# Small adds and the first batch's routing on GpSimd, four low parts of run 0's weight chunks on VectorE, in a fused attention, expert and feed-forward kernel

## The chip, the core and the metric

One core of one Trainium2 chip. The metric is the device time of one execution in microseconds (us); the time of a kernel is the median of its runs. TensorE (PE) does the matrix products and transposes, VectorE (DVE) and ScalarE (ACT) the elementwise work, GpSimd (POOL) elementwise work out of SBUF and the indirect DMAs, SyncE (SP) issues the other DMAs. Each engine takes its instructions in program order and waits on semaphores for the others.

## What is computed

Three layers behind each other. Attention: 2 batches of 8 heads, 576 positions, head size 64, with rotary embedding of q and k. Then a mixture of 8 experts over the 1152 tokens of 512 values, of which each token takes two. Then a feed-forward layer with softplus. The routing of the experts, on which this change bears, is

```
logits = x @ w_gate
noise_scale = np.log1p(np.exp(x @ w_noise))
noisy_logits = logits + noise_scale * noise
top2 = np.argpartition(-noisy_logits, 2, axis=1)[:, :2]
...
h = np.maximum(x[mask] @ w1[e], 0.0)
out[mask] += top2_w[mask, k, None] * (h @ w2[e])
```

## The kernel before, in words

**The attention stage** takes 16 heads g (8 per batch, batch 0 first) in 8 pairs p. A head has five row blocks, so there are 80 blocks n. For each, PE makes the scores S (L462), DVE the row maximum M (L475), ACT the exponential E with the row sums (L483). PE transposes the result (T, L496 to L508), ACT writes the high part of the transpose (L518) and DVE the rest as low part (L448). PE multiplies by the values (A, L532), ACT copies that out (L540 to L543), and PE forms X (L554): the head's output rows and its share of the 16 logits of every token. DVE scales X by the reciprocal row sum into `lgt` (L564) and `xs` (L573); the reciprocal comes from `row_sum` (L559, L560), two DVE instructions on 128x5 values for each head. Before a pair can start, its q and k are rotated on POOL (`rope_op`, ten instructions, L366 to L395) and transposed on PE (prep, L422 to L433), and its values are split on POOL (L402, L403).

**The routing** of batch 0 runs inside the attention of batch 1, as steps of the generator `route(0)` between two yields each, nearly all on DVE: sums over the heads (`presum`, L586, L587), softplus (L683 to L687), the two largest of 8 logits (L692 to L697), `Mt` and `Ms0`, which mark and count the chosen experts (L699, L702), counts over tokens on PE (RP, L706), positions (L718 to L732), `choose` for the expert of run 0 (L603 to L608), keys, indicator tiles `ohA` (L748) and `ohB` (L751, L753), a second product on PE (RP2, L758) and the index lists (L762, L763). `choose_rest` on POOL (L612 to L619) ends with `ordA`, the number of the expert of run 0, which SP must read before it can load that expert's weights. With `idxA` POOL gathers the rows of run 0 (`gather_A`, L919); PE transposes them (XT, L938).

**Weights.** `load_chunk` (L152) brings a chunk of 512 KB into one of four `wraw` buffers. `split_hi` (L170, ACT) writes its high part; the second half, queued in `lo_q`, subtracts it for the low part (L174) and then issues the next load into a free buffer. Run 0 needs eight chunks; the first six are split inside the attention stage, their low parts on POOL. Chunks 4 and 5 can be loaded only when the buffers of chunks 0 and 1 are free, that is when their low parts are done.

**After attention**, PE does run 0: `gemm1` (L250 to L252), between its halves the counts of the other batches' routing (`route(1)`, on DVE from L672), then `gemm2`, then a branch on `mxi` (L1284), and runs 1 to 8 and the feed-forward layer follow.

**The order of the attention stage** is made when the kernel is built. Each step is an `op` with a key, an engine, an assumed cost in ns, a place, and the steps it comes after; the table `AHEAD` shifts the place of each kind. `schedule` takes steps one by one, always the one that can start soonest by the assumed costs, lower place first, and writes out their instructions in that order. Two rows that matter later:

```
op(("rs", g), "DVE", 300, n - 3, [("E", 5 * g + 4)], row_sum, g)
op(("sl", i), "POOL", 2300, 100, [("sp", i)], lambda: lo_q.pop(0)())
```

Of the kernel before, what the change touches and what calls it, by code (L numbers as in the profile page):

```python
# [103 lines left out]
def fused_kernel(ctx: ExitStack, tc: tile.TileContext, q, k, v, w_gate, w_noise, noise, w1, w2,  # L104
# [55 lines left out]
    def split_hi():  # L160
# [8 lines left out]
        lo_eng = nc.gpsimd if s < NWA else nc.vector  # L169
# [413 lines left out]
    def presum(b):  # L583
        V = nc.vector
        if b == 0:
            V.tensor_reduce(out=Lx, in_=lgt[:, 4].rearrange("p h o -> p o h"), axis=AX.X, op=OP.add)  # L586
            V.tensor_reduce(out=L0, in_=lgt[:, 0:4].rearrange("p t h o -> p t o h"), axis=AX.X, op=OP.add)  # L587
        else:
            V.tensor_reduce(out=L1, in_=lgt[:, 5:10, 0:H - 2].rearrange("p t h o -> p t o h"), axis=AX.X, op=OP.add)
            V.tensor_tensor(out=L1[:, 0], in0=L1[:, 0], in1=Lx, op=OP.add)  # L590
            V.tensor_tensor(out=L1, in0=L1, in1=lgt[:, 5:10, H - 2], op=OP.add)

# [7 lines left out]
    def choose():  # L600

        V = nc.vector
# [55 lines left out]
    def route(b, pool):  # L658
        t0, t1 = (0, 4) if b == 0 else (4, NT)
# [4 lines left out]
        def tmp(name, shape, dt=F32):  # L664
            return pool.tile([128] + shape, dt, name=f"{name}{b}")

        if b == 0:
            presum(b)
            L = L0
        else:  # L670
            L = L1
            V.tensor_tensor(out=L, in0=L, in1=lgt[:, 5:10, H - 1], op=OP.add)  # L672
# [40 lines left out]
        if b == 0:  # L713
            nc.tensor.matmul(ps[:, NT, :], ones, Ms0, start=True, stop=True)
# [12 lines left out]
        if b:  # L727
            V.scalar_tensor_tensor(out=kc, in0=ps[:, NT, :], scalar=8.0, in1=kb2, op0=OP.mult, op1=OP.add)
            rank_steps = ranks(pool)
            next(rank_steps)  # L730
        else:
            V.scalar_tensor_tensor(out=kA, in0=ps[:, NT, :], scalar=8.0, in1=kb, op0=OP.mult, op1=OP.add)  # L732
            yield
            choose()
            yield
        V.tensor_tensor(out=pr, in0=oh[:, ts], in1=(tbB if b else tbA)[:, None, None, :].to_broadcast([128, T, 2, E]),
                        op=OP.mult)
# [811 lines left out]
```

## Time and profile before

| what | value |
|---|---|
| median of 3 runs | 676.83 us (675.26 to 677.0) |
| the profiled execution's own time | 676.09 us |
| its span, first to last instruction | 674.3 us |
| busy share of the span: PE, DVE, ACT, POOL | 94%, 76%, 64%, 34% |
| TensorE's granted clock, mean | 0.994 |

The profile is one execution. Its times count from the span's start. The attention stage lies from 0 to about 198 us. PE's busy time takes in the tails of its matmuls, so short waits of PE are hidden in it.

### The profile page before, as it was taken

How to read it: one execution, taken by the hardware profiler on the slowest of the kernel's cores; microseconds unless marked ns; L12 is line 12 of the kernel's file. 1: busy time of each engine (PE TensorE's matmuls, PEld its weight loads, DVE VectorE, ACT ScalarE, POOL GpSimd, SP SyncE). 2: the span in 40 equal slices, each digit the busy share in tenths (PEclk: the TensorE clock that was granted, in tenths of full speed). 3: DMA queues.
4: the chain of work that ended last, by engine and by line, in shares of the span. 5: the costliest groups of instructions: out<-in, count | busy, mean ns of one | idle time of the engine just before them, and what ended most of it. 6: DMA issues, size and time to landing. Idle time of an engine off the chain costs nothing.

```text
span 674.3 us, 11714 instructions
## 1 busy us (share of the span) xinstructions
PE 636.9 (94%) x4066; PEld 569.7 (84%) x4066; DVE 509.9 (76%) x1063; ACT 432.8 (64%) x912; POOL 228.4 (34%) x241
## 2 busy tenths in 40 slices
PE   3999999889998999999999999988999999999997
PEld 2798989878987888979888898977789999889996
DVE  7889899999986558768677768655997655676665
ACT  2887888678873547747575765645876544565553
POOL 6968966772365301432313241322120100000000
PEclk9999999999999999999999999998999999999999
DMA  6318421001441868998999899884520100100000
GB/s 157 92 44 308 137 56 55 1 19 55 144 130 55 289 216 261 322 345 282 354 303 315 290 315 318 279 311 126 157 60 35 33 17 0 48 2 1 32 1 31
DMA packets 67901, 101.08 MB, mean 150 GB/s; under 512 B 11232, under 2 KB 38624, under 8 KB 67840
## 3 DMA queue, kind: packets, MB, share of 16 engines
q1 hardware_dynamic: 61552, 84.59, 38.5%
q0 software_dynamic: 3136, 10.10, 4.6%
q10 hardware_dynamic: 3152, 5.62, 2.2%
q8 instruction: 33, 0.54, 0.3%
q14 instruction: 28, 0.23, 0.1%
HBM read 76.70 MB, written 23.59 MB: 149 GB/s over the span
## 4 chain that ended last, share of the span: by engine, by line
PE 62%; issue 2%; DMA 2%; DVE 1%; ACT 0%; POOL 0%; POOLq 0%; DVEq 0%
PE p L250 10%; PE p L251 10%; PE p L252 10%; PE ph L250 5%; PE po L252 5%; PE ph L251 5%; PE ph L252 5%; PE po L251 5%; PE po L250 5%; PE p L1117 2%; PE p L1119 2%; PE pa L1073 1%; DMA yg<-ytab,yrow 1%; DMA ytab<-y 1%; PE px L1366 0%
## 5 line engine op out<-in xcount | busy, mean ns | idle before, releaser
L174 DVE TENSOR_TENSOR w<-wraw,w 128x1024 fp32r<-128x1024 f32 x69 | 93.8, 1370 | 1.2 <-ACT w L170 1.2
L219 POOL TENSOR_TENSOR dm<-dm,da 128x512 int32<-128x512 int32 x32 | 42.0, 1314 | 134.0 <-DVE da L216 57.0
L170 ACT ACTIVATE w<-wraw 128x1024 fp32r<-128x1024 f32 x75 | 78.7, 1055 | 7.9 <-DMA wraw<-in_moe_w_dram 7.2
L251 PE MATMUL p<-xl,w 128*128 128x320 f32 (+3 forms) x256 | 77.5, 303 | 0.3 <-DVE xl L1076 0.3
L250 PE MATMUL p<-xh,w 128*128 128x320 f32 (+3 forms) x256 | 77.4, 302 | 0.0
L252 PE MATMUL p<-xh,w 128*128 128x320 f32 (+3 forms) x256 | 77.3, 302 | 0.0
L1427 ACT ACTIVATE fa<-ph 128x256 f32<-128x256 f32 (+1 forms) x64 | 26.0, 407 | 69.6 <-PE ph L252 69.5
L483 ACT ACTIVATE P<-ps,nmx 128x576 f32<-128x576 f32 (+1 forms) x80 | 59.2, 740 | 13.0 <-DVE nmx L475 11.9
L475 DVE TENSOR_REDUCE nmx<-ps 128x1 f32<-128x576 f32 (+1 forms) x80 | 60.0, 751 | 7.3 <-PE ps L462 5.8
L250 PE MATMUL ph<-xh,w 128*128 128x256 f32 (+1 forms) x192 | 58.4, 304 | 1.7 <-DVE xl L1372 1.4
L518 ACT ACTIVATE pth<-pt 128x512 fp32r<-128x512 f32 (+2 forms) x96 | 53.5, 569 | 9.3 <-PE pt L496 5.1
L250 PE MATMUL p<-w,hb 128*128 128x512 f32 x144 | 58.7, 408 | 0.0
L252 PE MATMUL ph<-xh,w 128*128 128x256 f32 (+1 forms) x192 | 57.4, 299 | 0.0
L251 PE MATMUL ph<-xl,w 128*128 128x256 f32 (+1 forms) x192 | 57.3, 299 | 0.0
L1093 DVE SCALAR_TENSOR_TENSOR hb<-p,hb 128x256 fp32r<-128x256 f32 (+1 forms) x104 | 31.7, 345 | 32.9 <-ACT hb L1089 32.8
L252 PE MATMUL p<-w,hb 128*128 128x512 f32 x144 | 56.6, 393 | 0.0
L251 PE MATMUL p<-w,hb 128*128 128x512 f32 x144 | 56.5, 393 | 0.0
L1434 DVE TENSOR_SCALAR fu<-fa 128x256 f32<-128x256 f32 (+1 forms) x64 | 19.8, 309 | 47.2 <-ACT fa L1428 46.9
L448 DVE TENSOR_TENSOR ptl<-pt,pth 128x512 fp32r<-128x512 f32 (+1 forms) x80 | 49.5, 628 | 2.0 <-ACT pth L518 1.5
L1347 POOL DMA_INDIRECT yg<-ytab,yrow x18 | 18.9, 1048 | 92.5 <-PE px L1366 71.6
L251 PEld LDWEIGHTS p<-xl,w 128*128 128x128 f32 x256 | 48.2, 188 | 0.8 <-DVE xl L1076 0.5
L250 PEld LDWEIGHTS p<-xh,w 128*128 128x128 f32 x256 | 48.2, 188 | 0.6 <-ACT xh L1075 0.2
(291 smaller groups left out, 1899.3 us busy)
## 6 DMA issues: line engine op xcount, KB each, us to landing
wraw<-in_moe_w_dram SPq DMA_DIRECT2D x64, 512.0 KB
x<-in_moe_w_in_dram SPq DMA_DIRECT2D x16, 512.0 KB
x<-in_moe_w_out_dram SPq DMA_DIRECT2D x16, 512.0 KB
wtab<-dm SPq DMA_DIRECT2D x32, 256.0 KB
wraw<-wtab SPq DMA_DIRECT2D x16, 512.0 KB
ytab<-y ACTq DMA_DIRECT2D x18, 256.0 KB
ytab<-zrow SPq DMA_DIRECT2D x1, 4096.0 KB
w<-in_v_dram SPq DMA_DIRECT2D x8, 256.0 KB
```

The source lines that it names most:

```text
L170: nc.scalar.activation(hi, r, AF.Copy)
L174: lo_eng.tensor_tensor(out=lo, in0=r, in1=hi.bitcast(F32), op=OP.subtract)
L219: nc.gpsimd.tensor_tensor(out=m, in0=m, in1=ai, op=OP.add)
L250: nc.tensor.matmul(ps, ah, bh, start=first and i == 0, stop=False)
L251: nc.tensor.matmul(ps, ah, bl, start=False, stop=False)
L252: nc.tensor.matmul(ps, al, bh, start=False, stop=last and i == n - 1)
L448: nc.vector.tensor_tensor(out=dl, in0=x, in1=dh.bitcast(F32), op=OP.subtract)
L475: nc.vector.tensor_reduce(out=nmx[p0:p1], in_=stS[n][p0:p1, :, :HN], axis=AX.XY, op=OP.max, negate=True)
L483: nc.scalar.activation(Pt[p0:p1, 0:S].rearrange("p (a c) -> p a c", a=2), ps[p0:p1, :, :HN], AF.Exp, bias=nmx[p0:p1], scale=1.0, accum_out ...
L518: nc.scalar.activation(*evac.pop(("T", g, u)), AF.Copy)
L1093: nc.vector.scalar_tensor_tensor(out=o, in0=ps[:, c], scalar=0.0, in1=hh[:, c].bitcast(F32), op0=OP.max, op1=OP.subtract)
L1427: nc.scalar.activation(a, ps, AF.Abs)
```

## The change

GpSimd now does the add of `row_sum` (the reciprocal stays on VectorE as `row_inv`), both `presum` functions (as trees of adds in place in `lgt`), and of the routing of batch 0 the softplus arithmetic, `Mt` and `Ms0`, `choose` after the maximum, the keys and both indicator tiles, of which it writes 8 and 8 rows with one instruction each. VectorE keeps the largest-two search and what reads PSUM. `route` now serves the other batches alone and is as before. Of run 0's first six low parts GpSimd keeps two and VectorE takes four. The chunk loads come after `choose_rest` instead of after the last routing step, and the first two high parts no longer wait for the last rotation. The rotation is given to the scheduler in nine pieces instead of one. `AHEAD` is unchanged.

```diff
-        lo_eng = nc.gpsimd if s < NWA else nc.vector
+        lo_eng = nc.gpsimd if s < 2 else nc.vector
...
     def row_sum(g):
         b, h = divmod(g, H)
-        nc.vector.tensor_scalar(rinv[:, b, :, h], sums[:, b, :, h], 1e-9, None, op0=OP.add)
+        nc.gpsimd.tensor_scalar(rinv[:, b, :, h], sums[:, b, :, h], 1e-9, None, op0=OP.add)
+
+    def row_inv(g):
+        b, h = divmod(g, H)
         nc.vector.reciprocal(rinv[:, b, :, h], rinv[:, b, :, h])
...
+        g = nc.gpsimd
+        t = lgt[:, 5 * b:5 * b + 5]
         if b == 0:
-            V.tensor_reduce(out=Lx, in_=lgt[:, 4].rearrange("p h o -> p o h"), axis=AX.X, op=OP.add)
-            V.tensor_reduce(out=L0, in_=lgt[:, 0:4].rearrange("p t h o -> p t o h"), axis=AX.X, op=OP.add)
+            g.tensor_tensor(out=t[:, :, 0:4], in0=t[:, :, 0:4], in1=t[:, :, 4:8], op=OP.add)
+            g.tensor_tensor(out=t[:, :, 0:2], in0=t[:, :, 0:2], in1=t[:, :, 2:4], op=OP.add)
+            g.tensor_tensor(out=L0, in0=t[:, 0:4, 0], in1=t[:, 0:4, 1], op=OP.add)
+            g.tensor_tensor(out=Lx, in0=t[:, 4, 0], in1=t[:, 4, 1], op=OP.add)
...
-        V = nc.vector
-        V.scalar_tensor_tensor(out=kA, in0=kA, scalar=8.0 * CAPS[0] + 8.0, in1=kA, op0=OP.is_lt, op1=OP.mult)
-        V.tensor_reduce(out=topA, in_=kA, axis=AX.X, op=OP.max)
-        V.tensor_scalar(isA, kA, topA[:, 0:1], None, op0=OP.is_equal)
...
+        g = nc.gpsimd
+        g.tensor_scalar(isA, kA, topA[:, 0:1], None, op0=OP.is_equal)
...
+    def route_first(pool):
...
+        g.tensor_scalar(c_, e_, 1.0, 1.0, op0=OP.add, op1=OP.subtract)
+        g.tensor_tensor(out=c_, in0=e_, in1=c_, op=OP.subtract)
+        g.tensor_tensor(out=l_, in0=l_, in1=c_, op=OP.add)
+        g.tensor_tensor(out=l_, in0=l_, in1=nz[:, ts], op=OP.mult)
+        g.tensor_tensor(out=nl, in0=l_, in1=L0[:, :, 0:8], op=OP.add)
...
+        g.tensor_tensor(out=Mt[:, ts], in0=oh[:, ts, 0], in1=oh[:, ts, 1], op=OP.add)
...
+                g.tensor_scalar(ohA[:, i, kk, :], iotaA, pmf[:, i, kk:kk + 1], None, op0=OP.is_equal)
...
+                g.tensor_scalar(ohB[:, i, kk, :], iotaB, key[:, i, kk:kk + 1], tval[:, i:i + 1], op0=OP.is_equal,
+                                op1=OP.mult)
...
-        op(("rs", g), "DVE", 300, n - 3, [("E", 5 * g + 4)], row_sum, g)
+        op(("rs", g), "POOL", 260, n - 8000, [("E", 5 * g + 4)], row_sum, g)
+        op(("ri", g), "DVE", 190, n - 60, [("rs", g)], row_inv, g)
...
-    op(("cr", 0), "POOL", 2300, 100, [("R", 7)], choose_rest)
+    op(("cr", 0), "POOL", 2300, 100, [("R", 8)], choose_rest)
...
-        op(("ld", i), "SP", 1500, 70 + i, [("Xd", 9), last[0]], load_chunk)
+        op(("ld", i), "SP", 1500, 70 + i, [("Xd", 9), ("cr", 0)], load_chunk)
...
-        op(("sl", i), "POOL", 2300, 100, [("sp", i)], lambda: lo_q.pop(0)())
-    op(("L", 0), "DVE", 1060, 80, [("Xd", 14)], presum, 1)
+        op(("sl", i), *(("POOL", 2400) if i < 2 else ("DVE", 1250)), 100, [("sp", i)], lambda: lo_q.pop(0)())
+    op(("L", 0), "POOL", 1700, 80, [("Xl", 14), ("R", 0)], presum, 1)
```

How the change moves instructions shows best at three places. The first is POOL's queue from the end of `choose_rest` on, as it was before (`wraw` is a loaded chunk, `w0` to `w5` the split chunks, `w5` also the gathered rows):

```order
L617 CAST ordA_90<-rank1_113 128x1
L618 TENSOR_SCALAR kb2_110<-isA_106 128x8
L619 TENSOR_TENSOR kb2_110<-kb2_110,kb_99 128x8
L919 DMA w5_2410<-xtab_60,idxA_87 128x512
L919 DMA w5_2410<-xtab_60,idxA_87 64x512
L174 TENSOR_TENSOR w0_2477<-wraw_2413,w0_2477 128x1024
L174 TENSOR_TENSOR w1_2565<-wraw_2443,w1_2565 128x1024
L174 TENSOR_TENSOR w2_2624<-wraw_2475,w2_2624 128x1024
```

and as it is with the change:

```order
L625 CAST ordA_90<-rank1_113 128x1
L626 TENSOR_SCALAR kb2_110<-isA_106 128x8
L627 TENSOR_TENSOR kb2_110<-kb2_110,kb_99 128x8
L559 TENSOR_SCALAR rinv_151<-sums_150 128x5
L736 TENSOR_SCALAR ohA0_2348<-iotaA_118,pmf0_2318 128x128 x8
L740 TENSOR_SCALAR ohB0_2349<-iotaB_119,key_84,tval_120 128x30 x8
L742 TENSOR_TENSOR dl8_80<-m80_2000 128x4
L559 TENSOR_SCALAR rinv_151<-sums_150 128x5
L990 DMA w5_2546<-xtab_60,idxA_87 128x512
L990 DMA w5_2546<-xtab_60,idxA_87 64x512
L174 TENSOR_TENSOR w0_2542<-wraw_2416,w0_2542 128x1024
L174 TENSOR_TENSOR w1_2588<-wraw_2453,w1_2588 128x1024
```

Sixteen indicator rows now stand between `ordA` and the gather, and two low parts instead of six behind it. On PE, RP comes after the scores of block 68 where it came after those of block 55, and RP2 after block 75 where it came after block 70.

The second place is ACT at the end of the attention stage, before (`P1` is the exponential of the last block, `pth` the high parts of transposes, `o0` and `o1` the outputs of the last two heads):

```order
L483 ACTIVATE P1_153,sums_150<-ps_2633,nmx_2647 64x576
L542 ACTIVATE o0_147<-pa_2649 128x224
L543 ACTIVATE o0_147<-pa_2649 128x64
L518 ACTIVATE pth_2593<-pt_2665 64x512
L518 ACTIVATE pth_2593<-pt_2670 128x4x128
L170 ACTIVATE w3_2688<-wraw_2499 128x1024
L518 ACTIVATE pth_2593<-pt_2691 128x5x64
L170 ACTIVATE w4_2714<-wraw_2512 128x1024
L540 ACTIVATE o1_148<-pa_2697 128x288
L170 ACTIVATE w5_2732<-wraw_2583 128x1024
L542 ACTIVATE o1_148<-pa_2721 128x224
L543 ACTIVATE o1_148<-pa_2721 128x64
```

and with the change:

```order
L483 ACTIVATE P1_153,sums_150<-ps_2631,nmx_2642 64x576
L170 ACTIVATE w2_2661<-wraw_2486 128x1024
L542 ACTIVATE o0_147<-pa_2650 128x224
L543 ACTIVATE o0_147<-pa_2650 128x64
L518 ACTIVATE pth_2624<-pt_2665 128x5x64
L518 ACTIVATE pth_2624<-pt_2672 128x4x128
L170 ACTIVATE w3_2694<-wraw_2508 128x1024
L540 ACTIVATE o0_147<-pa_2682 128x288
L170 ACTIVATE w4_2700<-wraw_2579 128x1024
L170 ACTIVATE w5_2711<-wraw_2608 128x1024
L518 ACTIVATE pth_2624<-pt_2713 128x4x128
L518 ACTIVATE pth_2624<-pt_2719 128x4x128
```

Four high parts of chunks instead of three now follow the last exponential, and all four stand ahead of the last two transposes' high parts.

The third place is DVE at the same point with the change (`pth` and `ptl` with a `pt` are the low parts of transposes):

```order
L174 TENSOR_TENSOR w2_2661<-wraw_2486,w2_2661 128x1024
L448 TENSOR_TENSOR ptl_2625<-pt_2672,pth_2624 128x4x128
L448 TENSOR_TENSOR ptl_2625<-pt_2665,pth_2624 128x4x64
L448 TENSOR_TENSOR pth_2624<-pt_2665,pth_2624 64x64
L174 TENSOR_TENSOR w3_2694<-wraw_2508,w3_2694 128x1024
L174 TENSOR_TENSOR w4_2700<-wraw_2579,w4_2700 128x1024
L567 TENSOR_TENSOR lgt_143<-pa_2705,rinv_151 128x5x16
L448 TENSOR_TENSOR ptl_2625<-pt_2713,pth_2624 128x4x128
L448 TENSOR_TENSOR ptl_2625<-pt_2719,pth_2624 128x4x128
L576 TENSOR_TENSOR xs_2744<-pa_2705,rinv_151 128x5x64
L174 TENSOR_TENSOR w5_2711<-wraw_2608,w5_2711 128x1024
```

None of the L174 rows stood on DVE in this stage before; three of the four are ahead of the last transposes' low parts.

## Rows read from the trace of the kernel before

**Rows 1.** Stretches, start:end, length; busy us and instructions of PE, PEld, DVE, ACT, POOL

```profile
34.00:51.00 17.00, 17.00 (x141) 16.45 (x140) 14.92 (x31) 14.12 (x37) 11.63 (x17) 1.00 0.18 51
...
54.30:114.07 59.77, 57.06 (x463) 54.42 (x462) 54.72 (x103) 49.44 (x125) 44.15 (x35) 1.00 0.42 138
114.07:171.34 57.27, 50.19 (x397) 45.48 (x395) 55.76 (x129) 42.31 (x104) 32.48 (x34) 1.00 0.16 49
```

**Rows 2.** Timeline of DVE, start and duration: one add of the routing

```profile
123.02 1.29 DVE L685 TENSOR_TENSOR l<-l,c 128x32 f32<-128x32 f32 x1
```

**Rows 3.** DVE in the eleven stretches that hold only moved instructions; last their sum

```profile
115.87:117.09 1.22, 1.22 (x3) 1.00 0.60 169
...
169.75:170.62 0.87, 0.81 (x3) 1.00 0.87 254
sum 11.88, DVE 11.43; mean DVE 1.04
```

**Rows 4.** Groups of DVE from 114.07 to 171.34 us: busy us, mean ns

```profile
L559 DVE TENSOR_SCALAR rinv<-sums 128x5 f32<-128x5 f32 x4 | 2.7, 663 | 0.0
...
L607 DVE TENSOR_TENSOR tbA<-isA,dA 128x8 f32<-128x8 f32 x1 | 1.4, 1383 | 0.0
...
L560 DVE RECIPROCAL rinv<-rinv 128x5 f32<-128x5 f32 x4 | 0.8, 191 | 0.1
...
L608 DVE TENSOR_TENSOR tbA<-tbA,base 128x8 f32<-128x8 f32 x1 | 0.2, 167 | 0.0
```

**Rows 5.** Groups from 0 to 270 us, all engines: busy us, mean ns, idle before

```profile
L518 ACT ACTIVATE pth<-pt 128x512 fp32r<-128x512 f32 (+2 forms) x96 | 53.5, 569 | 9.3 <-PE pt L496 5.1 <-PE pt L508 2.6 <-PE pt L500 1.1
...
L170 ACT ACTIVATE w<-wraw 128x1024 fp32r<-128x1024 f32 x23 | 24.3, 1056 | 2.9 <-DMA wraw<-in_moe_w_dram 2.8
L174 DVE TENSOR_TENSOR w<-wraw,w 128x1024 fp32r<-128x1024 f32 x17 | 21.9, 1300 | 0.0
...
L559 DVE TENSOR_SCALAR rinv<-sums 128x5 f32<-128x5 f32 x16 | 7.4, 460 | 1.4 <-ACT P L483 1.3
```

**Rows 6.** Groups of POOL over the whole span, shapes apart

```profile
L174 POOL TENSOR_TENSOR w<-wraw,w 128x1024 fp32r<-128x1024 f32 x6 | 14.2, 2389 | 11.2 <-ACT w L170 11.2
...
L1099 POOL TENSOR_TENSOR hb<-h,hb 128x128 fp32r<-128x128 f32 x6 | 2.8, 474 | 1.9 <-ACT h L1097 1.9
...
L619 POOL TENSOR_TENSOR kb<-kb,kb 128x8 f32<-128x8 f32 x1 | 0.2, 202 | 0.1
```

**Rows 7.** Timeline of POOL, start, duration, idle before with its releaser

```profile
122.80 1.47 POOL L384 TENSOR_TENSOR w<-w,w 128x576 f32<-128x576 f32 x1
...
125.56 1.46 POOL L395 TENSOR_TENSOR yg<-w,yg 128x576 fp32r<-128x576 f32 x1
...
172.56 1.24 POOL L919 DMA_INDIRECT w<-xtab,idxA  x1 [8.65 <-DVE dl L766]
174.09 0.91 POOL L919 DMA_INDIRECT w<-xtab,idxA  x1 [0.30 <-issue]
177.37 2.38 POOL L174 TENSOR_TENSOR w<-wraw,w 128x1024 fp32r<-128x1024 f32 x1 [2.37 <-ACT w L170]
```

**Rows 8.** Timeline of PE, start, duration, idle before with its releaser

```profile
136.13 0.63 PE L422 MATMUL pa<-ident,w 128*128 128x128 f32 x4
...
196.64 1.13 PE L554 MATMUL pa<-Wx,o 128*128 128x96 f32 x8 [0.90 <-ACT o L543]
...
204.21 0.20 PE L706 MATMUL pa<-Mt,tri 128*128 128x48 bf16 x1 [0.85 <-DVE Mt L699]
...
218.21 0.52 PE L1073 MATMUL pa<-ident,xg 128*128 128x128 f32 x3 [2.23 <-PEq L1284]
```

**Rows 9.** Timeline of ACT: the last exponential

```profile
189.97 0.74 ACT L483 ACTIVATE P<-ps,nmx 64x576 f32<-64x576 f32 x1
```

**Rows 10.** Stretches behind the first low part of a chunk, columns as in rows 1

```profile
181.20:183.20 2.00, 1.71 (x14) 1.47 (x14) 1.94 (x4) 1.98 (x7) 0.00 (x0) 1.00 0.67 250
183.20:187.00 3.80, 3.80 (x32) 3.57 (x31) 3.76 (x10) 3.62 (x9) 2.38 (x1) 1.00 0.00 0
```

More of the change, by code (lines that the diff above doesn't have):

```diff
@@ L660, in route @@
+    def route(pool):
+        t0, t1 = 4, NT
         T = t1 - t0
@@ L664, in tmp @@
         def tmp(name, shape, dt=F32):
[L665 to L672, printed above, removed]
+            return pool.tile([128] + shape, dt, name=f"{name}1")
+        L = L1
+        V.tensor_tensor(out=L, in0=L, in1=lgt[:, 5:10, H - 1], op=OP.add)
         e_ = tmp("e_", [T, E])
@@ L699, in route @@
         V.tensor_tensor(out=Mt[:, ts], in0=oh[:, ts, 0], in1=oh[:, ts, 1], op=OP.add)
-        if b == 0:
-            with nc.allow_low_precision("small integers, exact in bfloat16"):
-                V.tensor_reduce(out=Ms0, in_=Mt[:, 0:4].rearrange("p t e -> p e t"), axis=AX.X, op=OP.add)
         yield
         ps = psA.tile([128, NT + 1, E], F32, name="pa")
-        tn = t1 if b == 0 else NT + 1
+        tn = NT + 1
         nc.tensor.matmul(ps[:, t0:tn, :], tri, Mt[:, t0:tn, :], start=True, stop=False)
-        if b:
-            nc.tensor.matmul(ps[:, t0:tn, :], ones, Ms0[:, None, :].to_broadcast([128, tn - t0, E]), start=False,
-                             stop=False)
+        nc.tensor.matmul(ps[:, t0:tn, :], ones, Ms0[:, None, :].to_broadcast([128, tn - t0, E]), start=False,
+                         stop=False)
         for i in range(t0, tn - 1):
@@ L726, in route @@
         V.tensor_copy(out=pmf, in_=posm[:, ts])
[L727 to L737, printed above, removed]
+        V.scalar_tensor_tensor(out=kc, in0=ps[:, NT, :], scalar=8.0, in1=kb2, op0=OP.mult, op1=OP.add)
+        rank_steps = ranks(pool)
+        next(rank_steps)
+        V.tensor_tensor(out=pr, in0=oh[:, ts], in1=tbB[:, None, None, :].to_broadcast([128, T, 2, E]), op=OP.mult)
         ov = tmp("ov", [T, 2])
@@ L760, in route @@
         yield
-        if b == 0:
-            V.tensor_copy(out=idx0, in_=ps2)
-            V.tensor_copy(out=idxA, in_=ps2[:, E * CB:E * CB + RTILES[0]])
-        else:
-            V.tensor_tensor(out=idx, in0=ps2, in1=idx0, op=OP.add)
-        V.tensor_tensor(out=dl8[:, ts], in0=m8[:, :, 1], in1=m8[:, :, 0], op=OP.subtract)
-        if b:
-            yield
-            next(rank_steps)
-            yield
-            next(rank_steps)
+        V.tensor_tensor(out=idx, in0=ps2, in1=idx0, op=OP.add)
+        V.tensor_tensor(out=dl8[:, ts], in0=m8[:, :, 1], in1=m8[:, :, 0], op=OP.subtract)
+        yield
+        next(rank_steps)
+        yield
+        next(rank_steps)
     def later(pool):
@@ L985, in fused_kernel @@
         if p:
-            op(("rope", p), "POOL", 12800, n - 8, [("prep", p - 1, u) for u in range(5)] +
-               [("lp", p)] * (p > 2) if p > 1 else [("in", 0)], rope_op,
-               p)
+            after = [("prep", p - 1, u) for u in range(5)] + [("lp", p)] * (p > 2) if p > 1 else [("in", 0)]
+            pieces = list(rope_pieces(p))
+            for j, (cost, fn) in enumerate(pieces):
+                name = ("rope", p) if j + 1 == len(pieces) else ("ro", p, j)
+                op(name, "POOL", cost, n - 8 + (AHEAD["rope1" if p == 1 else "rope"] if j + 1 < len(pieces) else 0),
+                   after, fn)
+                after = [name]
         op(("vs", p), "POOL", 2850, n - 8, [("A", 2 * p - 3, 1), ("lv", p)] if p > 1 else [("in", 1)], vs_op, p)
```

130 lines of the change are left out of this document (98 added, 32 removed).

## The prediction

> **What bounds the kernel now.** The profile's page puts the end of the kernel on PE, so a gain has to come from PE waiting less. I looked at the busy time by stretches for the place where PE is less busy than elsewhere. In the attention stage between 54.30 and 114.07 us PE is busy 57.06 of 59.77 us and DVE 54.72; between 114.07 and 171.34 us, where the routing of batch 0 runs, PE falls to 50.19 of 57.27 us while DVE is busy 55.76 [rows 1]. The reader is to see that DVE has no time left there (97%) and that ACT, with 42.31, and POOL, with 32.48, have plenty. So DVE sets the pace of that stretch.
>
> Next I looked at what DVE does there. The group view shows small adds of very different price: 167 ns for one on 128x8, 1383 ns for its neighbour on the same shape [rows 4]. The timelines of DVE and POOL side by side say why: the add that starts at 123.02 us lasts 1.29 us, to 124.31, and a POOL instruction that was already running ends at 122.80 + 1.47 = 124.27 [rows 2, 7]. A small DVE instruction that reads and writes SBUF alone waits there for POOL's current one. The reciprocal, 191 ns on average, does not [rows 4].
>
> **What leaves DVE.** The sums over the heads, the softplus arithmetic, the marks, the choice, the keys and the indicator tiles fill eleven stretches of DVE's timeline with 11.88 us together [rows 3]. The four adds of `row_sum` in this stage add 2.7 us [rows 4]. That is 14.6 us of 57.27. What stays on DVE for the routing (the search for the largest two, the instructions that read PSUM) is moved later in the order and costs the same.
>
> What it is worth is set by the next engine. PE runs 397 instructions in the stretch. In the stretch before it ran 463 in 59.77 us, 0.129 us each [rows 1]; at that rate 397 take 51.2 us. Sixteen of them are the small products RP and RP2; without any charge for them it is 49.2. So the stretch would shrink by 6.0 to 8.1 us; **I take 7.2**. DVE alone would allow more: 55.76 - 14.6 = 41.2 us of work at the 92% of the stretch before is 45 us. The upper end is the densest stretch of the stage, 141 instructions in 17 us [rows 1], 0.121 each: 381 of them take 46 us, a gain of 11.3. The lower end is that ACT's and DVE's waits for each other keep half of it, 3.6.
>
> The other twelve adds of `row_sum` cost 7.4 - 2.7 = 4.7 us [rows 4, 5], spread over stretches where PE is 95% busy. **I take 1.0**, between 0 and 4.7, nearer the low end because little of PE's time is free there.
>
> **What POOL takes on.** Some 45 small instructions in the stretch, with no row of their own; the nearest are 202 ns for 128x8 and 474 ns for 128x128 [rows 6], so 9 to 21 us; most are of the small kind, and I take 13. With 32.48 us of its own POOL then holds 46 of about 50 us at most. That is covered as long as the rotation stays early: before, the rotation of pair 6 ended at 125.56 + 1.46 = 127.0 us and PE first used it at 136.13, 9 us later [rows 7, 8]. The two adds of `row_sum` per pair wait on POOL for an exponential, and the rotation is queued behind them; they and the sums over the heads take some 2 to 4 us of those 9. Cost nothing; if the cover went, each us would be a us of PE.
>
> An instruction of 128x1024 takes 2389 ns on POOL and 1300 on DVE [rows 5, 6], a factor of 1.8; for 128x8 it is 202 ns on POOL against 167 to 1383 on DVE [rows 4, 6]. The Trainium skill, page "GPSIMD Engine Reference", section "4.1 Engine selection", puts elementwise work on VectorE because GpSimd is about twice as slow with two inputs; by it this change would be wrong for the adds and right for the low parts, and the rows bear it out for the large shape only.
>
> **The end of the stage.** The first transposed rows of run 0 and the first low parts keep their kind and come later in the order. Four low parts go to DVE at 1.30 us [rows 5], 5.2 us, and lie in DVE's gaps while ACT works; the last sums over the heads, which DVE did there, go to POOL. The path is ACT's. Before, from the last exponential at 189.97 us to the last head's X at 196.64 passed 6.7 us [rows 8, 9], with one chunk's high part ahead of the last transpose's. Now there are four: three more, 3 x 1.06 = 3.2 us [rows 5], of which one stood ahead of the exponential before, so the stage ends 2.1 us later. **I take +2.1**, between 0 (if they fit into ACT's waits) and 4.5 (3.2 and one low part of DVE ahead of the last transposes).
>
> Behind the stage PE waited 0.85 us for the marks of the other batches [rows 8]. The sums they need are now done early on POOL, so **-0.85**. The 2.23 us that PE waits at the branch [rows 8] hang on PE's own products and stay. The loads of the chunks are issued when `ordA` is known, as before; run 0 has its weights in time in both cases.
>
> **Sum**: -7.2 - 1.0 + 2.1 - 0.85 = -6.95. The profiled execution took 676.09 us, so 669.1; the median of the runs shown, 676.83, is 0.74 above it, so the time to expect is **669.9 us**. No working behind the stage changes.
>
> **Rivals.**
>
> *PE at its densest.* If ACT's and POOL's slack let PE run the stretch as densely as it does early on, the gain is 11.3 there and up to 2.8 for `row_sum`, and the tail costs nothing: 676.83 - 15 = 662. For it: DVE is left with 73% of the stretch. Against it: even where no routing ran, from 54.30 to 114.07 us, PE did not keep that rate.
>
> *Given back at the end.* The order table is unchanged though the steps are others; if the stretch gives 3.6 us and the tail takes 4.5, the sum is about 0: 677. For it: ACT is full behind the last exponential. Against it: the gain lies ahead and is larger than any delay I can count there.
>
> *POOL becomes late* (slower). RP stands after block 68 now and RP2 after 75; between them POOL must do some 23 small instructions, an add of `row_sum` and the 16 indicator rows, 39 x 0.2 to 0.47 us = 8 to 18 us [rows 6], while PE has seven blocks, at 196.64/80 = 2.5 us each about 17 us. Behind that stand the gather, 2.45 us from 172.56 on, two low parts of 2.39, and only then the loads of chunks 4 and 5, which took until 183.20 after a low part that ended at 179.75, 3.5 us [rows 6, 7, 10]: 10.7 us, which ACT needs within some 14. So it decides once an indicator row costs 0.8 us or more; at 1.4 us the chain is 15 us late against my estimate, 12 behind the margin, and the kernel takes 676.83 - 7 + 12 = 682 us. Against it: no small POOL row is above 474 ns. If POOL took twice DVE's time for all that is moved, 2 x 14.6 and its own 32.48 make 62 us in a stretch that now takes 57.27, and the result is about the same 682. The Trainium skill's factor of two, in the section named above, would make it so; the rows of small instructions speak against it.
>
> *The change does not do what it says* is excluded for the placement: the orders show it.
>
> **How the numbers follow.** About 0.3%, 2 us, is what a measurement of this kernel can tell from no change. Forecast 0.60 (667 to 674.5), densest 0.15, given back 0.13, POOL late 0.12. Faster: 0.60 + 0.15 and a few hundredths of the third, 0.77; same 0.11; slower 0.12. The range goes from the densest case, 662, to the middle of "given back", 676, and leaves out about 2 in 10.
>
> **What would show it.** Right: the stretch of the routing has PE at 95% again and DVE near 85 to 90%; `row_sum`, the softplus and `choose` stand on POOL at 0.2 to 0.3 us each; PE does not wait at RP or RP2; the last X is some 6 us earlier than 196.64; the 0.85 us wait is gone. Wrong: waits of PE at RP2 or at the gathered rows' transposes for POOL, ACT waiting for a chunk's load, indicator rows of about 1 us, or a stage end that has not moved though DVE is free.

## The result and the profile after

The changed kernel takes 669.75 us, the median of 4 runs (667.85 to 671.74), against 676.48 us (675.26 to 677.0) in the same session: a ratio of 0.9901, with a 95% interval from 0.9882 to 0.992. The prediction was 669.9 us in a range from 662 to 676. On another chip session the same kernel took 670.81 us (ratio 0.9913, 0.9891 to 0.9936). The profiled execution is a long one of its kernel: 671.74 us, with a span of 669.9 against 674.3 before.

The answer to [rows 1] is the same two stretches of the changed kernel (columns as there; the last three numbers are the granted clock, the busy share of the DMA engines and GB/s):

```profile
54.30:114.07 59.77, 58.57 (x477) 55.98 (x476) 51.48 (x99) 50.73 (x128) 48.79 (x48) 1.00 0.46 147
114.07:171.34 57.27, 54.68 (x441) 51.52 (x440) 48.10 (x106) 47.25 (x118) 46.72 (x79) 1.00 0.17 53
```

In the stretch of the routing PE is busy 54.68 us where it was 50.19, and runs 441 instructions instead of 397; DVE is at 84% instead of 97%, and POOL took 14 us more. The stretch before it gained too, 477 instructions instead of 463.

What PE waited for in the stretch of the routing (us in total, times, longest; the first two rows of each list), before:

```profile
PE pt L508 <- DVE pth L448: 1.9, 1, 1.9
PE ps L462 <- ACT P L483: 1.7, 1, 1.7
...
```

and with the change:

```profile
PE pt L500 <- DVE ptl L448: 0.8, 1, 0.8
PE pa L747 <- POOL ohB L740: 0.5, 2, 0.3
...
```

The whole lists come to 7.1 us before, 5.4 of them for DVE, and to 2.3 us now, 1.5 of them for DVE.

What the moved work costs on POOL, by group (busy us, mean ns of one), to be held against [rows 4, 6]:

```profile
L736 POOL TENSOR_SCALAR ohA<-iotaA,pmf 128x128 f16<-128x128 f16 x8 | 4.7, 606 | 0.1
L559 POOL TENSOR_SCALAR rinv<-sums 128x5 f32<-128x5 f32 x16 | 3.8, 241 | 21.0 <-ACT P L483 18.1 <-PE ps L462 2.7
L740 POOL TENSOR_SCALAR ohB<-iotaB,key,tval 128x30 f16<-128x30 f32 x8 | 3.7, 481 | 0.0
...
L615 POOL TENSOR_TENSOR tbA<-isA,dA 128x8 f32<-128x8 f32 x1 | 0.2, 205 | 0.0
```

Most small rows cost 0.20 to 0.26 us, the longest 0.35; the adds of the sums over the heads, which are wider (up to 128x320), cost 0.22 to 1.34 us. `tbA` for example, which had lasted 1383 ns on DVE because POOL was busy, is 205 ns. The sixteen indicator rows cost 0.48 and 0.61 us each, more than any POOL row in [rows 6] but the low parts. The sixteen adds of `row_sum` come with 21 us in which POOL does nothing but wait, most of them for the exponential; experiment 1 comes back to them.

The timeline of PE (start, duration, idle before and releaser), at RP2 and at the end of the attention stage:

```profile
170.44 0.17 PE L747 MATMUL pa<-ohB,ohA 128*128 128x30 f16 x1 [0.23 <-POOL ohB L740]
...
180.92 0.37 PE L532 MATMUL pa<-pth,vhl 128*128 128x288 f32 x1 [1.23 <-DVE yg L448]
...
185.32 1.13 PE L554 MATMUL pa<-Wx,o 128*128 128x96 f32 x8 [0.54 <-ACT o L540]
...
187.69 0.40 PE L532 MATMUL pa<-pth,vhl 128*128 128x288 f32 x1 [0.37 <-ACT pth L518]
188.50 0.40 PE L534 MATMUL pa<-ptl,vhl 128*128 128x288 f32 x1 [0.41 <-DVE ptl L448]
...
191.65 1.35 PE L554 MATMUL pa<-Wx,o 128*128 128x96 f32 x10 [0.62 <-ACT o L543]
192.78 0.33 PE L250 MATMUL p<-yg,w 128*128 128x192 f32 x1
...
212.31 1.08 PE L1149 MATMUL pa<-ident,xg 128*128 128x128 f32 x4 [2.04 <-DVEq L1360]
```

Against [rows 8]: the last X starts at 191.65 us instead of 196.64, 5.0 us earlier; the branch is passed at 212.31 instead of 218.21, 5.9 us earlier, since the wait for the marks is gone. At RP2 PE goes at the pace at which POOL writes `ohB`, four short waits of 1.05 us together. And behind the last exponential, which is now at 180.79 us, there are four short waits for ACT and DVE, 1.94 us together, where the kernel before has two (0.37 us in front of the X at 191.34 and the 0.90 of [rows 8]). A longer one stands just ahead of them: at 180.92 us PE has waited 1.23 us for `yg`, the low part of the transposed rows of run 0, on DVE. The kernel before has no such wait.

Of the 5.9 us the profiled execution keeps 4.4 at its end. The rest is lost about 455 us, where nothing was changed. There PE waits for gathered rows (2.05, 1.92 and 1.41 us between 447 and 455 us), and the granted clock falls to 1.2 GHz (half) afterwards. The stretches of this execution and of another one of the same kernel (the run "changed again" below), columns as in rows 1:

```profile
454.00:456.00 2.00, 0.63 (x3) 0.63 (x4) 0.69 (x1) 0.59 (x1) 0.95 (x1) 0.67 0.01 4
456.00:458.00 2.00, 2.00 (x11) 2.00 (x11) 0.00 (x0) 0.00 (x0) 1.62 (x2) 0.50 0.63 147
458.00:460.00 2.00, 2.00 (x11) 2.00 (x10) 0.64 (x2) 1.60 (x4) 1.23 (x2) 0.50 0.75 197
460.00:462.00 2.00, 2.00 (x14) 2.00 (x13) 1.16 (x4) 1.54 (x4) 0.00 (x0) 0.63 0.61 188
```

```profile
454.00:456.00 2.00, 0.59 (x5) 0.35 (x4) 0.69 (x1) 0.60 (x1) 0.00 (x0) 0.96 0.34 131
456.00:458.00 2.00, 2.00 (x10) 2.00 (x11) 0.00 (x0) 0.00 (x0) 1.65 (x2) 0.50 0.18 35
458.00:460.00 2.00, 2.00 (x14) 2.00 (x14) 0.20 (x1) 1.07 (x3) 1.39 (x3) 0.69 0.73 223
460.00:462.00 2.00, 2.00 (x19) 2.00 (x18) 1.47 (x5) 1.88 (x5) 0.76 (x1) 1.00 0.69 178
```

Summing what is missing to 1.00 over the stretches of 2 us gives the time lost to the clock: 3.4 us in the first, 1.7 in the second, 1.7 in the kernel before at the same place. So the one execution of the changed kernel loses 1.7 us more there than its other, and the 1.5 us are no fixed price of the change. The executions of experiments 2 and 6 show 3.4 us at this place as well, that of experiment 3 nothing, the rest 1.7.

### The profile page after: what moved, and what is told of

It reads as the page before. It is cut to its first block, busy times and chain, and to the rows that moved or that the text cites. A ratio compares the mean times of both kernels' runs of the same rounds, so it can differ in the third digit from the quotient of the medians.

```text
span 669.9 us, 11791 instructions
## 1 busy us (share of the span) xinstructions
PE 636.3 (95%) x4066; PEld 571.1 (85%) x4066; DVE 490.5 (73%) x1018; ACT 432.3 (65%) x912; POOL 242.1 (36%) x307
## 4 chain that ended last, share of the span: by engine, by line
PE 60%; DMA 3%; issue 2%; DVE 2%; ACT 1%; POOL 0%; DVEq 0%; POOLq 0%; SPq 0%
PE p L250 9%; PE p L251 9%; PE p L252 9%; PE ph L250 5%; PE po L252 5%; PE po L251 5%; PE po L250 5%; PE ph L252 5%; PE ph L251 5%; DMA wraw<-wtab 2%; PE p L1193 2%; PE p L1195 1%; PE pa L1149 1%; DMA yg<-ytab,yrow 1%; PE px L1442 0%
## 5 line engine op out<-in xcount | busy, mean ns | idle before, releaser
L174 DVE TENSOR_TENSOR w<-wraw,w 128x1024 fp32r<-128x1024 f32 x73 | 98.3, 1358 | 1.4 <-ACT w L170 1.2
L448 DVE TENSOR_TENSOR ptl<-pt,pth 128x512 fp32r<-128x512 f32 (+1 forms) x80 | 49.4, 631 | 4.4 <-ACT pth L518 3.8
```

What stands on the lines that cost most here:

```text
L174: lo_eng.tensor_tensor(out=lo, in0=r, in1=hi.bitcast(F32), op=OP.subtract)
L448: nc.vector.tensor_tensor(out=dl, in0=x, in1=dh.bitcast(F32), op=OP.subtract)
```

## The experiments

Theory: DVE was the bound of the routing's stretch; taking the small adds off it is the gain. Rivals: the new order of steps brings it (the scheduler now sees the rotation in nine pieces), `row_sum` brings it, or the low parts and loads do. In kernels called "same order", the scheduler still plans as in the change and only the engine of the emitted instruction differs, so PE and ACT have the instructions of the change in the same order.

All are summed up here. A ratio is taken to the kernel before in the same session. "Run 0" is the start of run 0's first product on PE in the profile; "clock" is the time lost to the clock from 34 us on, summed as above, the last 4 us of the span left out. Both come from one execution each: the two of the changed kernel start run 0 1.0 us apart, so a difference of 1 us in that column shows nothing by itself.

| kernel | median us | ratio to before (95%) | run 0 | clock |
|---|---|---|---|---|
| before | 676.5 | | 197.78 | 3.4 |
| changed | 669.75 | 0.9901 (0.9882 to 0.992) | 192.78 | 5.1 |
| changed again | 670.81 | 0.9913 (0.9891 to 0.9936) | 193.78 | 3.4 |
| routing on DVE, same order | 672.58 | 0.9954 (0.9939 to 0.9969) | 196.05 | 1.7 |
| `row_sum` on DVE, same order | 670.10 | 0.9914 (0.9899 to 0.9928) | 193.65 | 3.4 |
| both on DVE, same order | 683.10 | 1.0109 (1.0094 to 1.0124) | 208.45 | 6.8 |
| routing on DVE, planned anew | 689.06 | 1.0183 (1.016 to 1.0207) | 211.40 | 8.5 |
| rotation in one piece | 672.86 | 0.996 (0.9945 to 0.9974) | 196.28 | 5.1 |
| before, rotation in pieces | 684.02 | 1.0132 (1.0115 to 1.0149) | 206.91 | 6.8 |
| all low parts on POOL | 670.52 | 0.9907 (0.9881 to 0.9932) | 191.21 | 5.1 |
| chunks 2 to 5 split late | 668.80 | 0.9883 (0.9866 to 0.99) | 190.94 | 3.4 |
| chunks 2 to 5 late, 5 last | 667.54 | 0.9871 (0.9849 to 0.9894) | 191.94 | 1.7 |
| loads late | 672.54 | 0.9958 (0.994 to 0.9975) | 193.90 | 6.8 |
| true indicator costs | 674.05 | 0.9967 (0.9949 to 0.9985) | 196.99 | 6.8 |

**1. The routing back on DVE, in the same order.**

```diff
     def route_first(pool):
...
-        V, g = nc.vector, nc.gpsimd
+        V = g = nc.vector
```

and the same in `choose` and in `presum` for batch 0.

> Same order of all steps as the changed kernel, only the engine differs: the first batch's routing arithmetic (sums over its heads, softplus, marks, choice, keys, both indicator tiles) runs on DVE again; row_sum and the low parts stay as changed. Theory (the engine is what counts, the stretch was bound by DVE): 674 to 678 us, PE busy in the stretch 114 to 171 us back near 50 to 51 of 57 us, single adds of 1.2 to 1.4 us on DVE again. Rival (the gain comes from the new order of steps, above all the rotation in nine pieces): 669 to 671 us, PE stays at 54 to 55 of 57.

672.58 us, between the two expectations: +2.8 against the change. PE runs 417 instructions in the stretch of the routing instead of 441, 50.96 us of DVE are busy. But the single adds, which should have been slow again, were not:

```profile
135.48 0.19 DVE L681 TENSOR_TENSOR c<-e,c 128x32 f32<-128x32 f32 x1
```

The timeline of POOL of the same kernel says why, it is idle then:

```profile
131.59 1.55 POOL L403 TENSOR_TENSOR vhl<-w,vhl 128x640 fp32r<-128x640 f32 x1
137.36 0.24 POOL L559 TENSOR_SCALAR rinv<-sums 128x5 f32<-128x5 f32 x1 [4.22 <-ACT P L483]
```

POOL's next instruction is a `row_sum` that waits for an exponential, and the next rotation is queued behind it. The slots that the scheduler had kept on POOL for the routing stay empty, so none of the moved instructions stalls on DVE; only a cast that the change too has there (L692) takes 1.44 us instead of 0.30. What is left is the work itself: the 24 instructions that PE runs less are 3.1 us at 0.13. Part of the price may be hidden in the total, since at the branch this kernel's clock did not fall, 1.7 us less lost than the kernel before at that place. To the start of run 0 the routing on DVE costs 196.05 - 192.78 = 3.3 us, or 2.3 against the other execution of the changed kernel.

**2. `row_sum` back on DVE, in the same order.**

```diff
-        nc.gpsimd.tensor_scalar(rinv[:, b, :, h], sums[:, b, :, h], 1e-9, None, op0=OP.add)
+        nc.vector.tensor_scalar(rinv[:, b, :, h], sums[:, b, :, h], 1e-9, None, op0=OP.add)
```

> The changed kernel in its own order of steps, with the 16 adds of row_sum on DVE again. In the changed kernel the eighth head's logits are written at 110.06 us where they were at 113.81, a gain of 3.75 us ahead of the routing. Theory (these 3.75 us are the adds of row_sum that stood on DVE until POOL's current instruction ended): 672 to 674 us, eighth head back at 112.5 to 114 us, the adds at 0.4 to 0.7 us on DVE. Rival (the new order of steps brings them): 669 to 671 us, eighth head at 110 to 111 us.

670.10 us, no difference that shows, in the rival's range. The eighth head's logits are at 111.15 us: of the 3.75 us gained by then (113.81 to 110.06), the adds are about 1.1 and the new order about 2.65 (the changed kernel's other execution has 110.23). The adds do stall on DVE again, 524 ns on average (group of DVE, columns as in rows 4):

```profile
L559 DVE TENSOR_SCALAR rinv<-sums 128x5 f32<-128x5 f32 x16 | 8.4, 524 | 0.2
```

DVE has room for that while POOL does the routing.

**3. Both on DVE, in the same order.**

> Both on DVE in the changed kernel's order: the first batch's routing arithmetic and the adds of row_sum; low parts, loads and order as changed. Theory (each adds its own price): 672.6 us of the routing alone and 2 to 4 us for row_sum, 674.5 to 677 us, about the time of the kernel before. Rival (the order is most of the change): 671 to 673.5 us.

683.10 us: neither expectation. The two prices, 2.8 and about 0, do not add; together they are 13 us, and the new order without these two moves is 1.1% slower than the old kernel. So the order alone is not the gain. The reverse, the old order with the new engines, no run here shows. Without `row_sum` and the routing nothing of the moved work holds POOL back, so its rotation runs on just while DVE does the small adds. The timelines of DVE, POOL and PE at the softplus:

```profile
143.22 1.47 DVE L681 TENSOR_TENSOR c<-e,c 128x32 f32<-128x32 f32 x1
144.72 0.71 DVE L682 TENSOR_TENSOR l<-l,c 128x32 f32<-128x32 f32 x1
```

```profile
141.88 2.76 POOL L376 TENSOR_TENSOR w<-w,w 128x512 f32<-128x512 f32 x2
144.59 0.80 POOL L366 TENSOR_TENSOR w<-w,w 128x288 f32<-128x288 f32 x1
```

```profile
119.42 1.06 PE L500 MATMUL pt<-ident,P 128*64 128x128 f32 x4 [4.01 <-DVE ptl L448]
...
147.18 1.06 PE L500 MATMUL pt<-ident,P 128*64 128x128 f32 x4 [4.97 <-DVE ptl L448]
```

The add at 143.22 ends at 144.69, when POOL's pair of instructions ends (144.64); the same add took 0.19 us in experiment 1. PE waits 4.01 us behind the sums over the heads and 4.97 behind the softplus, for a low part of a transpose that is queued behind them on DVE. The sums take 3.98 us on DVE here and 1.20 in experiment 1, the softplus 4.15 and 1.08; PE's waits behind them are 1.23 and 1.90 us in experiment 1. So the stalls make up the difference. And about each of the long waits the granted clock goes to half:

```profile
118.00:122.00 4.00, 2.58 (x12) 2.47 (x13) 2.72 (x5) 1.19 (x2) 3.84 (x4) 0.55 0.00 0
122.00:126.00 4.00, 4.00 (x22) 3.82 (x21) 3.61 (x5) 1.78 (x5) 2.91 (x3) 0.60 0.00 0
...
146.00:150.00 4.00, 2.82 (x14) 2.71 (x15) 3.93 (x19) 1.20 (x3) 3.00 (x3) 0.50 0.00 0
150.00:154.00 4.00, 4.00 (x23) 4.00 (x23) 3.87 (x8) 1.05 (x3) 2.57 (x2) 0.68 0.02 4
```

The two waits and the clock, 4.0 + 5.0 + 6.8 = 15.8 us (the clock is down in the last part of each wait already, so a little is counted twice), are about the whole delay of run 0's start, 208.45 - 192.78 = 15.7 (14.7 against the other execution of the changed kernel).

**4. The routing on DVE, and the scheduler told so.**

```diff
-    stages = [("R", "POOL", 1700), ("R", "ACT", 385), ("R", "POOL", 1100), ...
+    stages = [("R", "DVE", 1700), ("R", "ACT", 385), ("R", "DVE", 1100), ...
```

> The same routing arithmetic on DVE, but the scheduler is told so and makes its order again. Theory: 672 to 677 us, a little less than with the order kept, since the order can make room; the rest of the change (row_sum, order, low parts) is then worth 0 to 4 us against the kernel before. Rival (order): 669 to 671 us.

689.06 us, above both expectations and 16.5 us worse than with the order kept. The scheduler's costs know nothing of POOL, so it puts the adds beside the rotation: `c<-e,c` lasts 1484 ns, and PE waits 7.7 us in six pieces for low parts of transposes (L448) and 2.6 us for a low part of k; 8.5 us go to the clock.

**5. Two orders made anew.** The rotation as one step in the changed kernel, and in pieces in the kernel before:

```diff
-            pieces = list(rope_pieces(p))
...
+            op(("rope", p), "POOL", 12800, n - 8, after, lambda p=p: [f() for _, f in rope_pieces(p)])
```

> The changed kernel with the rotation given to the scheduler as one step of 12.8 us again; the scheduler makes its order anew, POOL keeps all the small work. Theory (who does the work decides, the pieces don't): 668 to 672 us. Rival (the small work waits behind a whole rotation of about 13 us on POOL, and row_sum with it): 674 to 682 us, DVE waiting for sums or PE for the logits.

> The kernel before with one thing of the change: the rotation in nine pieces, order made anew, all small work on DVE. Theory (DVE is the bound and keeps its work): 675 to 679 us. Rival (the finer order alone brings the gain): 669 to 673 us.

672.86 us, just between the two expectations, and 684.02 us, worse than both. The pieces alone, with the small work on DVE, do harm. In the first, the last exponential is even earlier (179.97 us against 180.79), but the transposed rows of run 0 now stand in the end of the stage; PE stands 2.0 us in front of them for something that the trace does not name, the clock falls from 186 to 194 us, and the last X starts at 195.15. All other steps move too when the order is made anew, so these two runs show that an order is worth several us, not which of its places is.

**6. All six low parts on POOL.**

```diff
-        lo_eng = nc.gpsimd if s < 2 else nc.vector
+        lo_eng = nc.gpsimd if s < NWA else nc.vector
...
-        op(("sl", i), *(("POOL", 2400) if i < 2 else ("DVE", 1250)), 100, [("sp", i)], lambda: lo_q.pop(0)())
+        op(("sl", i), "POOL", 2400, 100, [("sp", i)], lambda: lo_q.pop(0)())
```

> All six low parts of run 0's chunks on POOL as before, everything else as changed. Theory (behind the last exponential ACT's high parts decide, DVE's low parts lie in gaps): 669 to 671 us, last X within 1 us of the changed kernel's 191.65. Rival (the four low parts on DVE are part of the gain, POOL at 2.38 us each holds chunks 4 and 5 back): 673 to 676 us, ACT waiting for a load or a low part.

670.52 us: as the theory has it, no difference. But two things cancel. The last X is 1.6 us earlier (190.07; within 1 us was expected): the order was made anew with this edit, and two chunks' high parts now stand ahead of the last transposes' on ACT instead of four. And 1.23 us are given back in a wait for the marks. The sums over the heads are done before the last X here too; what is late is an add of the softplus on DVE, which lasts until POOL's low parts end (189.77 + 4.71 = 194.48). DVE and POOL:

```profile
192.56 1.98 DVE L771 TENSOR_SCALAR c<-e 128x40 f32<-128x40 f32 x1 [0.30 <-ACT e L769]
```

```profile
189.77 4.71 POOL L174 TENSOR_TENSOR w<-wraw,w 128x1024 fp32r<-128x1024 f32 x2
```

In the changed kernel, where DVE has these low parts, the same add takes 0.19 us. So the engine of the low parts does matter, for the marks; what it is worth with the order kept, no run shows.

**7. Chunks 2 to 5 split behind the last transposes.**

```diff
-           prep7 * (i >= 4) + [("XTl", 0), ("XTl", 1)] * (i == 5), split_hi)
+           prep7 * (i >= 4) + [("XTl", 0), ("XTl", 1)] * (i == 5) + [("Th", 15, u) for u in range(6)] * (i > 1), split_hi)
```

> The changed kernel with the high parts of chunks 2 to 5 held until the last transposes' high parts are written. Theory (three high parts ahead of the last transposes cost the end of the stage 3 to 4 us): last X at 188 to 189 us instead of 191.65, 666 to 667.5 us. Rival (PE's own products and DVE's low parts set that end, or the weights then come late to run 0): 669 to 671 us.

668.80 us, between the two expectations. ACT's timeline in the changed kernel shows what stood in front: chunks 2 to 5 between 181.64 and 187.15 us, and the last transposes' high parts behind them.

```profile
180.79 0.74 ACT L483 ACTIVATE P<-ps,nmx 64x576 f32<-64x576 f32 x1
...
181.64 1.06 ACT L170 ACTIVATE w<-wraw 128x1024 fp32r<-128x1024 f32 x1
...
183.91 1.05 ACT L170 ACTIVATE w<-wraw 128x1024 fp32r<-128x1024 f32 x1
184.86 0.40 ACT L540 ACTIVATE o<-pa 128x288 f32<-128x288 f32 x1
185.15 2.00 ACT L170 ACTIVATE w<-wraw 128x1024 fp32r<-128x1024 f32 x2
187.05 1.08 ACT L518 ACTIVATE pth<-pt 128x512 fp32r<-128x512 f32 x2
```

With the chunks held back, PE's timeline has the last X at 189.80, 1.85 us earlier (3 to 4 were expected), and a new wait for the marks. The waits at 185.32, 187.69 and 188.50 us are gone, the 1.23 us for `yg` is still there:

```profile
189.80 1.35 PE L554 MATMUL pa<-Wx,o 128*128 128x96 f32 x10 [0.72 <-ACT o L543]
...
196.97 0.20 PE L791 MATMUL pa<-Mt,tri 128*128 128x48 bf16 x1 [0.46 <-DVE Mt L787]
```

**8. The same, with chunk 5 behind the softplus of the other batches.** As 7, and:

```diff
-    for i in range(NWA):
+    for i in range(NWA - 1):
...
-    for _ in range(3):
-        next(r1)
+    next(r1)
+    split_hi()
+    for _ in range(2):
+        next(r1)
+    split_lo()
```

> The changed kernel itself, as the yardstick for the other three on the same chip: 668.5 to 671 us. If its profiled execution again waits behind the experts at about 455 us, the 1.5 us that it lost there belong to the change; if not, they were that execution's own.

> The changed kernel with the high parts of chunks 2 to 4 held until the last transposes' high parts are written, and chunk 5 split behind the softplus of the other batches' routing (its low part behind their marks). Holding chunks 2 to 5 alone brought the last X from 191.65 to 189.80 us and left 0.46 us of waiting for the marks. Theory (that wait hangs on chunk 5's high and low part, which stood ahead of the softplus): wait at the marks under 0.1 us, 667.5 to 669 us, 1 to 2 us below the changed kernel of the same chip. Rival (PE is full there and the end is given back at the branch): within 0.7 us of it.

667.54 us against 670.81 of the changed kernel in the same session: 3.3 us less, the fastest version of the study (0.9871 of the kernel before). That is the lower edge of the theory's range, though a gain of 3.3 us is more than the 1 to 2 that it named. The wait at the marks is gone; run 0 starts 1.8 us earlier than in that execution. The rest is the clock's, and not safely this version's: the changed kernel too has executions with a mean clock of 0.997, 668.80 and 670.02 us, against 667.24, 667.27 and 668.67 here, which is about 1.7 us of difference. In the profiled executions PE waits 2.13 us at the branch, as the changed kernel does (2.04 in both), but the clock stays up behind it:

```profile
210.00:212.00 2.00, 0.53 (x5) 0.56 (x6) 0.42 (x2) 0.00 (x0) 0.45 (x2) 1.00 0.55 166
212.00:214.00 2.00, 2.00 (x10) 1.37 (x10) 0.69 (x1) 0.60 (x1) 1.49 (x6) 1.00 0.92 302
```

What makes the clock fall there in one execution and not in the other stays open.

**9. The loads late again.**

```diff
-        op(("ld", i), "SP", 1500, 70 + i, [("Xd", 9), ("cr", 0)], load_chunk)
+        op(("ld", i), "SP", 1500, 70 + i, [("Xd", 9), last[0]], load_chunk)
```

> The changed kernel with the chunk loads after the last routing step, as before, instead of after the choice. Theory (the chunks' loads have room, run 0 has its weights in time in both cases): within 1 us of the changed kernel. Rival (the earlier loads let the first high parts go ahead of ACT's full end of the stage, so four or five of them now crowd in front of the last transposes): 1.5 to 4 us slower, the last X at 193 to 195 us.

672.54 us, 1.7 above the changed kernel: the rival's size, by another way. SP now issues two of the first four loads only behind the transfers of x, from 176.42 us on. ACT then stands 1.99 us in front of a chunk, with the copy of the last head's output behind it, PE waits for that copy, and the clock falls:

```profile
190.27 1.06 ACT L170 ACTIVATE w<-wraw 128x1024 fp32r<-128x1024 f32 x1 [1.99 <-POOL L L600]
191.24 0.34 ACT L542 ACTIVATE o<-pa 128x224 f32<-128x224 f32 x1
```

```profile
191.74 2.45 PE L554 MATMUL pa<-Wx,o 128*128 128x96 f32 x10 [2.23 <-ACT o L543]
```

The releaser that is named, a sum on POOL, neither reads nor writes the chunk. The DMA engines become busy only at about 187 us (a share of 0.64 after 0.00), behind POOL's low part of the second chunk, which frees a buffer at 186.44 us here and at 179.77 in the changed kernel. So it was most likely the load.

**10. The indicator rows at their true cost in the plan.**

```diff
-              ("R", "POOL", 1400), ("R", "POOL", 2100), ("RP", "PE", 190), ("RF", "DVE", 330)]
+              ("R", "POOL", 2340), ("R", "POOL", 3870), ("RP", "PE", 190), ("RF", "DVE", 330)]
```

and 2340 for the first four rows.

> The changed kernel with the indicator rows entered in the scheduler's plan at what they took: 2340, 2340 and 3870 ns instead of 1400, 1400 and 2100. Theory (the order puts RP2 about 3.5 us too early for POOL; PE waited 1.05 us on four of its products, and stands at it for 1.7 us): no wait of PE at RP2, 668 to 670 us. Rival (the order behind it is made anew and its end is worse, as with other re-made orders): 671 to 675 us.

674.05 us: the theory's step is right and the rival has the total. PE no longer waits at RP2, and the last exponential is at 179.60 us, 1.7 us earlier than in "changed again". But the transposed rows of run 0 now fall into the end of the stage; PE waits there five times, 5.1 us together, the clock falls from 188 to 199 us (5.1 us lost), and the last X is at 194.84.

## Why the prediction was right, and where its terms were not

**The bound.** Right: DVE set the pace of the stretch, and PE took over. PE went to 95%, as written, DVE to 84% (85 to 90 was written), POOL to 46.7 us (46). PE's waits for DVE in the stretch went from 5.4 to 1.5 us. That DVE's adds stall until POOL's instruction ends, as read from one pair of rows [rows 2, 7], is what experiments 1 and 3 show with one and the same add: 0.19 us beside an idle POOL, 1.47 beside a busy one.

**The stretch, -7.2.** The rows say 441 instructions of PE instead of 397: 44 more at 57.27/441 = 0.13 us each is 5.7 us, inside the range of 3.6 to 11.3. PE's pace there, 0.130 us, is the one taken from the stretch before; what was left out are RP2's waits for POOL's indicator rows (1.05 us, 0.78 of them in this stretch). The upper end of 8.1 rests on sixteen small products in the stretch; the trace has thirteen (five of RP, eight of RP2), which makes it 7.7 and changes nothing else.

**`row_sum` elsewhere, -1.0.** Up to 114.07 us PE has run 760 instructions instead of 745, 1.9 us. The adds themselves are about the 1.0 that was taken (1.1 at the eighth head, experiment 2); the rest is the new order, which the sum had at nothing.

**The end of the stage, +2.1.** Of the 64 instructions by which PE has less to do behind 171.34 us (134 to run 0's start, 198 before), 8.3 us at 0.129, it is only 5.0 us shorter (21.44 us against 26.44): 3.3 lost, between 0 and 4.5 as bounded, 1.2 more than taken. The mechanism named, ACT's high parts, is there: held back, they give 1.85 us (experiment 7). Most of the rest, 1.23 us, is a wait that the prediction put at nothing: it said that the first transposed rows of run 0 come later in the order, and gave them no price. PE's product at 180.92 us waits until DVE has written their low part, 180.08 + 0.69 = 180.77 us:

```profile
180.08 0.69 DVE L448 TENSOR_TENSOR yg<-pa,yg 128x512 fp32r<-128x512 f32 x1
```

The same 1.23 us stand in the other execution of the changed kernel and in experiments 1 to 3 and 6 to 8.

**The marks, -0.85.** From run 0's start to its second half PE took 12.38 us and takes 11.69: -0.69. The size is right, the reason another. The add of the last head's logits to the sums, which the softplus waits for, is on DVE in both kernels. Before, it lasted until POOL's three low parts ended (193.40 + 7.07 = 200.47 us); DVE and POOL before:

```profile
198.70 1.87 DVE L672 TENSOR_TENSOR L<-L,lgt 128x80 f32<-128x80 f32 x1
```

```profile
193.40 7.07 POOL L174 TENSOR_TENSOR w<-wraw,w 128x1024 fp32r<-128x1024 f32 x3 [3.12 <-ACT w L170]
```

and DVE with the change:

```profile
193.60 0.23 DVE L764 TENSOR_TENSOR L<-L,lgt 128x80 f32<-128x80 f32 x1
```

So it is the low parts' leaving POOL that freed the marks, rather than sums done early; with the low parts on POOL again the wait is back although the sums are early (experiment 6).

**POOL, 0.** Nearly. PE never waited for a rotation from 34 us on. The indicator rows are 0.61 and 0.48 us where 0.2 to 0.47 was assumed; the point named from which POOL decides, 0.8 us, was not reached, and the forecast of no wait at RP2 was wrong by 1.05 us.

**Together**: -1.9 - 5.7 + 3.3 - 0.7 = -5.0 by the rows, against -5.9 measured at the branch and -6.95 forecast. Of the difference 0.2 us is the branch (2.04 us of waiting instead of 2.23), and the count is good to about 0.6 us, since the trace has 1340 instructions of PE up to run 0 before and 1335 now. Part of the agreement of the medians (669.75 and 669.9) is luck: two terms that were too small and two that were too large, and a clock that takes 1.7 us more or less in one execution or another. For the marks the reason was wrong as well.

**The rivals.** "Given back at the end" happened for 3.3 us, not for all. "POOL becomes late", with the factor of two for everything that is moved, did not: an add of 128x8 costs 0.20 to 0.21 us on POOL, where DVE takes 0.16 to 0.17 beside an idle POOL. For the indicator rows it is 606 ns on POOL against 250 on DVE (`ohA`) and 481 against 294 (`ohB`, both in experiment 1). So the rule of the Trainium skill, page "GPSIMD Engine Reference", section "4.1 Engine selection", that GpSimd is about twice as slow with two inputs, agrees with the rows for the low parts alone (2389 ns against 1300). The small adds speak against it, and there the rows decide; for the indicator rows, which read one tile and one value per row, it does not state that factor.

**What the prediction missed altogether** is that the two moves are not two prices. It took 7.2 us for the routing's stretch, four of the sixteen adds among it, and 1.0 for the other twelve adds, and added them up as if each stood alone. In this order each alone is worth 0 to 3 us and both together 13. The rows of experiments 1 to 3 suggest why: with `row_sum` on POOL, POOL happens to stand idle while DVE does the softplus; with the routing on POOL, DVE has room for the stalls of `row_sum`; with neither there, the stalls fall on a DVE that has no time. The order that the scheduler makes for the change is good only with the engines it was made for, and the 6.7 us are what that pair, order and engines, is better than the old pair, the low parts and loads included.

## What to carry to other kernels

Look beside each small instruction that takes several times its usual duration for what the other engine is doing at that moment; then the remedy is either to move it or to let it fall where the other engine waits, and here the two did not add up. Where a scheduler orders the steps, test an engine move with the order kept, or the order's own effect (up to 16.5 us here) hides the move's. And take away from the end of a stage what its successor needs late: run 0 then starts 1.8 us earlier here.

## What was not expected of the hardware

The granted clock fell to 1.2 GHz for some us about waits of PE: single ones of 1.6 to 5.0 us, or several close together (of 0.8 to 1.5 us in experiment 10). Each such time cost 1.7, 3.4 or 5.1 us in these executions; they make up 1.7 to 8.5 us of an execution, which is not small against the differences between the kernels. But the same wait at the branch, 1.9 to 2.3 us, was followed by a fall in some executions (before, both of the changed kernel, experiments 4, 6, 7 and 9) and not in others (1, 2, 3, 8, 10 and both of experiment 5).

The waiting between DVE and POOL goes both ways. An add of the sums over the heads on POOL (L598, 128x80) lasted 1.34 us in the changed kernel, from 182.83 us on, while DVE worked on a low part until 183.96; in experiment 6, with no low part on DVE, it took 0.36.

An instruction of `ohA` (a compare of 128x128 f16 with one value per row) took 606 ns on POOL and 250 ns on DVE, while an add of 128x8 takes about 200 on POOL and 160 to 170 on DVE when the other is idle.
